# Attention, soft mixture of experts and gated layer in one kernel: the first four heads loaded and scaled in two halves

## The chip, the cores and the metric

The kernel runs on one core of a Trainium2 chip. The metric is the device time of one execution in microseconds (us); the runs shown are executions of the same program, and their median is what is compared.

## The reference, cut to what matters

Three layers follow each other. The first is causal attention over 4 batches, 12 heads, 448 positions and 64 channels a head; its output is the token matrix x of 1,792 rows and 768 columns. The second is a soft mixture of 8 experts with 4 slots each; the third is a gated layer.

```python
scores = scale * np.matmul(q, k.transpose(0, 1, 3, 2))
scores = np.where(mask, -1000000000.0, scores)
scores = scores - np.max(scores, axis=-1, keepdims=True)
attn = np.exp(scores)
attn = attn / (np.sum(attn, axis=-1, keepdims=True) + 1e-09)
return np.matmul(attn, v).astype(np.float32)
...
logits = x @ phi
...
slot_input = d.T @ x
...
    h = np.maximum(slot_input[e] @ w1[e], 0.0)
    slot_out[e] = h @ w2[e]
...
return (c @ slot_out).astype(np.float32)
...
gate = 1.0 / (1.0 + np.exp(-(x @ w_gate)))
val = x @ w_val
return (gate * val @ w_out).astype(np.float32)
```

Here d and c are the softmax of the logits over the tokens and over the slots.

## The kernel before, in words

**The attention stage.** The 48 heads are taken in 24 pairs of two heads (indices i), and the pairs in 12 groups of four heads (indices g, two pairs each). The q, k and v of a group are loaded together: `load` (L270) issues one DMA for each of the four chunks of positions `CH` (128, 128, 128 and 64 rows), each bringing all four heads of the group, 256 bytes a row and head. All loads are issued by SP, in the order of the program. q and k have two buffers for the groups in turn (`qkbuf`, L263), and so has v (`vbuf`, L260).

Scores are computed in half precision from q and k split into a high and a low part. Before the split q and k are multiplied by a power of two, so that they fit. That power comes from the mean square of the group's q and k: `scales` (L287) sums the squares, averages them over the partitions with a small matmul by a constant matrix `avgb` (tile `psq`), and makes from it `qks`, the two factors for q and k, and `sc`, the factor for the scores, with four small DVE operations on `qkp`. For group 0 the squares are summed by one operation on DVE for q and one on ACT for k, each over all 1,024 columns of the group (tile `sq`, sums in `am`). For every later group POOL squares and adds in halves (tiles `sq`, `sqr`).

A pair then passes these steps: `st_T` (L336) transposes q and k on PE into PSUM (`psT`, four matmuls each); `st_hi` (L343) on ACT writes the high part `hi` with the scale; `st_lo` (L347) on DVE writes the rest, `lo`; `score` (L356) multiplies the parts on PE into `psS`, for the blocks of queries t = 0 to 3 (1 and the short last block 3, called Z, in one step, 2 and 0 in the next); `st_m` (L380) on DVE adds the mask, scales and takes the maximum `nm`; `st_e` (L392) on ACT takes the exponential `P` and its sum; `st_r` and `st_ri` (L399, L405) make the reciprocal `r` of the sums on POOL and DVE; `st_P` and `st_C` transpose P on PE (`psP`) and copy it to SBUF; `st_V` multiplies with v, and further steps normalise, transpose and multiply with `phi`.

**What sets the order.** The order in the attention stage is written out by hand: each step of each pair has a time in the table `AT` (L82), each load one in `LOADS` (L86), each part of `scales` one in `SCALES` (L87); `at` and `gen` (L584, L587) put them on a list, which is sorted by time and then written out (L627). `Pinned` (L235) keeps each instruction in this order on its engine; since it calls all of them, most rows of the attention stage carry its line, L244, and are told apart by their tiles. Only the order comes from the table; an instruction runs when its engine has done those before it and its inputs are there. For group 0 all loads and the whole scale stand before time 0, ahead of the transposes of pair 0. The exponential's table is loaded by the operation on `warm` (L626) ahead of the whole list.

**After the attention** a stage streams the experts' weights `w1`, `w2` in 1.5 MB pieces through a ring of buffers, of which ten pieces came during the attention (`load_w`, L173); then the gated layer runs in six parts: per part the weights are converted (`from_f64`, L186, on ACT and DVE; `prep`, L711), gates are computed (`gate`, L834) and the output products are added up in `oacc` (`outp`, L854). The order of these two stages is laid out by the scheduler, which starts from the whole program.

## Time and profile before

| what | value |
|---|---|
| runs | 594.41, 592.43, 593.85 us; median 593.85 |
| profiled execution | span 595.0 us, the time that it has |
| busy share of the span | PE 86%, DVE 66%, ACT 54%, POOL 40% |
| DMA | 101.59 MB, mean 171 GB/s |
| chain that ended last | PE 63%, ACT 15%, DMA 7%, DVE 5%, issue 3%, POOL 2% |

The profiled execution is one run of the program with the hardware profiler; its own time is the span, from the first instruction to the last, and it lies 1.2 us above the median of the runs. PE is TensorE's matmuls, PEld its weight loads, DVE VectorE, ACT ScalarE, POOL GpSimd, SP SyncE. An engine's busy share is taken over the whole span and mixes stages. The chain is followed back from the last instruction, at each step to what released it.

### The profile page before, as it was taken

The numbers are of one execution on the slowest core, as the hardware profiler recorded it, in microseconds if no ns is written. First come the engines' busy times: TensorE is split into PE (matmuls) and PEld (weight loads), VectorE is DVE, ScalarE is ACT, GpSimd is POOL, SyncE is SP. The second block draws the span as 40 slices with busy tenths as digits, with TensorE's granted clock in tenths as the row PEclk, the third lists the DMA queues.
The fourth block names the chain that finished last, engine by engine and source line by source line (L and its number), as shares of the span: only waits on it lengthen the run. The fifth ranks groups of instructions, "written<-read, shape, count | busy, mean of one in ns | idle before, by whom it ended". The sixth has DMA issues, their size and how long they took to land.

```text
span 595.0 us, 12947 instructions
## 1 busy us (share of the span) xinstructions
PE 514.5 (86%) x4971; PEld 317.2 (53%) x4971; DVE 390.0 (66%) x943; ACT 322.6 (54%) x738; POOL 238.7 (40%) x333
## 2 busy tenths in 40 slices
PE   2899989998999899799935689679999989899997
PEld 1576756665667566465512235344554445455654
DVE  3688877886878687331027038986895958675664
ACT  2577767776777577301043049996865843334300
POOL 6654663656365410000000014206696760355720
PEclk9899999999999899979995789998999979799999
DMA  7746557464774313779999993713505303000044
GB/s 161 200 106 170 167 160 199 129 144 133 199 196 115 91 33 107 287 251 391 405 397 405 405 400 137 281 38 119 200 1 209 110 2 107 0 1 1 2 185 186
DMA packets 95566, 101.59 MB, mean 171 GB/s; under 512 B 68625, under 2 KB 68625, under 8 KB 95505
## 3 DMA queue, kind: packets, MB, share of 16 engines
q1 hardware_dynamic: 95504, 100.77, 51.3%
q8 instruction: 39, 0.64, 0.5%
q14 instruction: 23, 0.18, 0.1%
HBM read 95.26 MB, written 5.51 MB: 169 GB/s over the span
## 4 chain that ended last, share of the span: by engine, by line
PE 63%; ACT 15%; DMA 7%; DVE 5%; issue 3%; POOL 2%; SPq 1%; ACTq 0%; DVEq 0%; POOLq 0%
PE pso L870 22%; PE psP L244 9%; PE psS L244 8%; DMA w<-in_moe_w_dram 6%; ACT P L244 4%; PE psX L244 4%; PE psT L244 4%; PE psh L762 3%; PE so L775 3%; ACT hi L244 3%; ACT oacc L144 2%; ACT w L194 2%; PE psg L688 2%; PE psg L843 1%; ACT w L144 1%
## 5 line engine op out<-in xcount | busy, mean ns | idle before, releaser
L852 POOL TENSOR_TENSOR hlo<-hs,hhi 128x448 f16<-128x448 f32 x48 | 59.2, 1241 | 174.9 <-DVE hhi L851 132.5
L870 PE MATMUL pso<-wh,hhi 128*128 128x384 f16 (+1 forms) x384 | 111.5, 338 | 8.1 <-ACT oacc L144 7.6
L870 PE MATMUL pso<-wl,hhi 128*128 128x384 f16 (+1 forms) x384 | 110.3, 334 | 0.0
L870 PE MATMUL pso<-wh,hlo 128*128 128x384 f16 (+1 forms) x384 | 107.8, 331 | 2.6 <-POOL hlo L852 2.6
L244 ACT ACTIVATE P<-psS,nm 128x256 f32<-128x256 f32 (+3 forms) x168 | 82.0, 504 | 31.4 <-PE psP L244 16.6
L870 PEld LDWEIGHTS <-hhi 128*128 128x128 f16 (+1 forms) x768 | 63.5, 103 | 63.8 <-issue 32.3
L244 DVE CUSTOM_DVE_ANT_0 psS<-psS,cmaskq,sc 128x256 f32<-128x256 f32 (+1 forms) x144 | 66.5, 489 | 32.7 <-PE psS L244 30.2
L882 DVE SCALAR_TENSOR_TENSOR oacc<-pso,osc,oacc 128x384 f32<-128x384 f32 x98 | 58.7, 613 | 35.1 <-PE pso L870 34.6
L244 PE MATMUL psP<-ident,P 128*128 128x128 f32 x384 | 59.6, 288 | 17.7 <-ACT P L244 11.6
L880 POOL TENSOR_TENSOR oacc<-oacc,ev 128x384 f32<-128x384 f32 x42 | 55.0, 1321 | 23.1 <-ACT ev L144 23.0
L244 PEld LDWEIGHTS psP<-ident,P 128*128 128x128 f32 x384 | 41.3, 142 | 35.9 <-ACT P L244 21.5
L244 POOL TENSOR_TENSOR sq<-sq 128x512 bf16<-128x512 bf16 (+1 forms) x88 | 56.3, 640 | 6.5
L244 PE MATMUL psV<-PT,v 128*64 128x64 f32 (+3 forms) x672 | 48.0, 293 | 0.3 <-ACT PT L244 0.3
L870 PEld LDWEIGHTS <-hlo 128*128 128x128 f16 (+1 forms) x384 | 34.1, 102 | 26.1 <-issue 3.5
L198 DVE SCALAR_TENSOR_TENSOR w<-w 128x1536 int32<-128x1536 int32 x18 | 33.7, 1874 | 14.5 <-ACT w L144 14.1
L244 PEld LDWEIGHTS psV<-PT,v 128*64 128x64 f32 x672 | 32.0, 137 | 20.9 <-issue 14.0
L144 ACT ACTIVATE ev<-pso,osc 128x384 f32<-128x384 f32 x42 | 23.6, 581 | 27.4 <-PE pso L870 23.7
L194 ACT ACTIVATE w<-w 128x1536 int32<-128x1536 uint16 x18 | 30.2, 1680 | 14.9 <-DMA w<-in_moe_w_out_dram 7.9
L244 POOL TENSOR_SCALAR r<-sum 128x7 f32<-128x7 f32 x24 | 5.9, 244 | 79.1 <-ACT P L244 71.9
L762 PE MATMUL psh<-w,slotT 128*32 128x256 f32 x384 | 29.9, 441 | 7.8 <-DMA w<-in_moe_w_dram 7.3
L244 ACT ACTIVATE hi<-psT,qks 128x448 f16<-128x448 f32 x48 | 27.8, 630 | 15.2 <-PE psT L244 15.2
L770 ACT COPY hT<-psht 128x256 f32<-128x256 f32 x8 | 3.0, 372 | 61.0 <-PE psht L768 61.0
(233 smaller groups left out, 1000.7 us busy)
## 6 DMA issues: line engine op xcount, KB each, us to landing
w<-in_moe_w_dram SPq DMA_DIRECT2D x32, 1536.0 KB, 9.3
w<-in_moe_w_out_dram SPq DMA_DIRECT2D x6, 1536.0 KB, 12.2
w<-in_moe_w_val_dram SPq DMA_DIRECT2D x6, 1536.0 KB, 13.4
w<-in_moe_w_gate_dram SPq DMA_DIRECT2D x6, 1536.0 KB, 6.7
out_dram<-oacc SPq DMA_DIRECT2D x14, 384.0 KB, 2.3
q<-in_q_dram SPq DMA_DIRECT2D x36, 128.0 KB, 3.0
k<-in_k_dram SPq DMA_DIRECT2D x36, 128.0 KB, 2.9
v<-in_v_dram SPq DMA_DIRECT2D x36, 128.0 KB, 8.0
```

Source lines behind the costliest of these rows:

```text
L144: nc.scalar.activation(out=out, in_=in_, func=AF.Copy, scale=x)
L194: nc.scalar.activation(out=lo, in_=top, func=AF.Copy, scale=2.0 ** -13, bias=2.0 ** -15 - 0.5)
L198: nc.vector.scalar_tensor_tensor(lo, hi, -2 ** 31, lo, ALU.bitwise_and, ALU.bitwise_or)
L244: x = f(*a, **kw)
L688: nc.tensor.matmul(ps[32 * g:32 * g + 32, :], lhsT=soT[:, kc], rhs=w[:, kc], start=kc < 4, stop=kc + 4 >= KC)
L762: nc.tensor.matmul(ps[32 * g:32 * g + 32, :], lhsT=slotT[:, kc, :], rhs=w[:, kc % 3, 256 * g:256 * g + 256], start=kc == 0, stop=kc == KC - 1)
L775: nc.tensor.matmul(so[32 * c:32 * c + 32, :], lhsT=hT[:, i, 32 * g:32 * g + 32], rhs=w[:, f % 4, 256 * c:256 * c + 256], start=e == 0 and ...
L843: nc.tensor.matmul(pg, lhsT=d["g"][:, cols], rhs=cT[:, b * S:(b + 1) * S], start=True, stop=True)
L852: nc.gpsimd.tensor_tensor(lo[:, c], hs, hi[:, c], ALU.subtract)
L870: nc.tensor.matmul(ps[n][o:o + m], lhsT=hid[b, u][x][:, c, s0:s0 + m], rhs=y[:, c, 384 * n:384 * n + 384], start=f, stop=l)
L880: nc.gpsimd.tensor_tensor(a, a, x, ALU.add)
L882: nc.vector.scalar_tensor_tensor(a, ps[n], osc, a, ALU.mult, ALU.add)
```

## The change

It touches the attention stage's start only.

- Group 0's q and k are no longer loaded with four heads a DMA. Heads 0 and 1 (o = 0) come first, with four DMAs for q on SP and four for k on ACT's queue, then heads 2 and 3 (o = 2) with eight DMAs on SP.
- `scales` for group 0 runs twice, once for each pair of heads, on half the columns: for o = 0 at times -16 and -15, for o = 2 at 7.0 and 9.4, which is inside pair 0. The squares are written to `vbuf[1]`, which no load has filled yet, in place of the tile `sq`. The steps read the scale of their own pair (`scale_of`).
- The transposes of pair 0 stand at -17, ahead of the first scale.
- The last two parts of group 1's scale stand 3 and 3.4 units later (-1.0 and 0.5 in place of -4.0 and -2.9, relative to that group).
- The table load for the exponential stands at -20 on ACT, behind the four DMA issues there.

```diff
--- before.py
+++ after.py
@@ -275,30 +275,38 @@
 
         def load_q(g):
             grp[g] = {"qk": qkbuf[g % 2]}
-            load(qkbuf[g % 2][0], q, g)
+            if g == 0:
+                for o in (0, 2):
+                    for w, src in enumerate((q, k)):
+                        for j, (s0, n) in enumerate(CH):
+                            (ac if w and not o else sp).dma_start(
+                                out=qkbuf[0][w][:n, j, o * D:(o + 2) * D].rearrange("p (h d) -> p h d", d=D),
+                                in_=src[0, o:o + 2, s0:s0 + n, :].rearrange("h p d -> p h d"))
+            else:
+                load(qkbuf[g % 2][0], q, g)
 
         def load_k(g):
-            load(qkbuf[g % 2][1], k, g)
+            if g:
+                load(qkbuf[g % 2][1], k, g)
 
         def load_v(g):
             grp[g]["v"] = vbuf[g % 2]
             load(vbuf[g % 2], v, g)
 
-        def scales(g):
+        def scales(g, o=None):
 
             n = 4 * HG * D
             if g == 0:
                 am = sm_p.tile([128, 2], F32, tag="am", name="am")
-                for i in range(2):
-                    x = grp[g]["qk"][i].rearrange("p j f -> p (j f)")
-                    sq = qk_p.tile([128, n], BF16, tag="sq", name="sq")
-                    if i:
-                        ac.activation(out=sq, in_=x, func=AF.Square, accum_out=am[:, i:i + 1])
-                    else:
-                        ve.tensor_tensor_reduce(out=sq, in0=x, in1=x, scale=1.0, scalar=0.0, op0=ALU.mult, op1=ALU.add,
-                                                accum_out=am[:, i:i + 1])
+                sq, sk = (vbuf[1].rearrange("p j f -> p (j f)")[:, n // 4 * i:n // 4 * i + n // 4].bitcast(BF16) for i in range(2))
+                j4 = lambda x: x.rearrange("p (j f) -> p j f", j=4)
+                x, y = (grp[g]["qk"][i][:, :, o * D:(o + 2) * D] for i in range(2))
+                ac.activation(out=j4(sk), in_=y, func=AF.Square, accum_out=am[:, 1:2])
+                ve.tensor_tensor_reduce(out=j4(sq), in0=x, in1=x, scale=1.0, scalar=0.0, op0=ALU.mult, op1=ALU.add,
+                                        accum_out=am[:, 0:1])
                 am16 = sm_p.tile([128, 2], BF16, tag="am16", name="am16")
                 ve.tensor_copy(am16, am)
+                yield
                 ps = psT.tile([128, 2], F32, tag="t", name="psq")
                 te.matmul(ps, lhsT=avgb, rhs=am16, start=True, stop=True)
                 mx = ps
@@ -330,8 +338,13 @@
             ve.tensor_scalar(p, p, 2.0 ** (64 + 3 - 14), 2.0 ** -34, ALU.mult, ALU.max)
             ve.reciprocal(s, p)
             ve.tensor_scalar(sc, p[:, 0:1], p[:, 1:2], -scale, ALU.mult, ALU.mult)
-            grp[g].update(s=s, sc=sc)
-            yield
+            for x in range(4) if o is None else (o, o + 1):
+                grp[g]["s", x], grp[g]["sc", x] = s, sc
+            yield
+
+        def scale_of(i, x="s"):
+            g, o = GOF[i]
+            return grp[g][x, o]
 
         def st_T(i, w):
 
@@ -342,12 +355,12 @@
 
         def st_hi(i, w):
             hi = pr[i]["hi", w] = qT_p.tile([128, S], F16, tag=f"hi{w}", name=f"hi{w}")
-            ac.activation(out=hi, in_=pr[i]["ps", w][:, :S], func=AF.Copy, scale=grp[GOF[i][0]]["s"][:, w:w + 1])
+            ac.activation(out=hi, in_=pr[i]["ps", w][:, :S], func=AF.Copy, scale=scale_of(i)[:, w:w + 1])
 
         def st_lo(i, w):
             d = pr[i]
             lo = d["lo", w] = qT_p.tile([128, S], F16, tag=f"lo{w}", name=f"lo{w}")
-            ve.scalar_tensor_tensor(lo, d.pop(("ps", w))[:, :S], grp[GOF[i][0]]["s"][:, w:w + 1], d["hi", w], ALU.mult, ALU.subtract)
+            ve.scalar_tensor_tensor(lo, d.pop(("ps", w))[:, :S], scale_of(i)[:, w:w + 1], d["hi", w], ALU.mult, ALU.subtract)
 
         def scores(i, ts):
             for t in ts:
@@ -386,7 +399,7 @@
             n = ps.shape[1]
             mask = cmask if t == NQ else cmaskq
             c = 2 * t + h
-            ve.tensor_tensor_reduce(out=ps, in0=ps, in1=mask[:, mask.shape[1] - n:], scale=grp[GOF[i][0]]["sc"],
+            ve.tensor_tensor_reduce(out=ps, in0=ps, in1=mask[:, mask.shape[1] - n:], scale=scale_of(i, "sc"),
                                     scalar=3.0e38, op0=ALU.add, op1=ALU.min, accum_out=d["nm"][:, c:c + 1])
 
         def st_e(i, t, h):
@@ -593,7 +606,7 @@
             t0 = II * i
             for w in range(2):
                 x = "qk"[w]
-                at(t0 + AT["T" + x], st_T, i, w)
+                at(t0 + AT["T" + x] if i else -17.0, st_T, i, w)
                 at(t0 + AT["h" + x], st_hi, i, w)
                 at(t0 + AT["l" + x], st_lo, i, w)
             at(t0 + AT["S20"], scores, i, (2, 0))
@@ -619,11 +632,15 @@
             at(t0 + LOADS["q"], load_q, g)
             at(t0 + LOADS["k"], load_k, g)
             at(t0 + LOADS["v"], load_v, g)
-            gen([t0 + x for x in SCALES], scales, g)
+            if g:
+                gen([t0 + x for x in (SCALES if g > 1 else SCALES[:-2] + (-1.0, 0.5))], scales, g)
+            else:
+                gen([-16.0, -15.0], scales, 0, 0)
+                gen([7.0, 9.4], scales, 0, 2)
             if 1 <= g <= NC + NA:
                 at(t0 + LOADS["w"], load_w)
+        at(-20.0, lambda: ac.activation(out=warm, in_=one1, func=AF.Exp))
         at(1.0, lambda: sp.dma_start(out=phis, in_=phi.rearrange("(k p) s -> p k s", p=128)))
-        nc.scalar.activation(out=warm, in_=one1, func=AF.Exp)
         for _, _, f, a in sorted(steps, key=lambda x: x[:2]):
             f(*a)
 
```

What this makes of the order of instructions is shown at three places.

*PE at the program's start.* `psq` is the averaging matmul (avgb its weights, am the sums of squares), `psT` the transposes of pair 0, `psS` its first scores. Before:

```order
L244 LDWEIGHTS avgb
L244 MATMUL psq<-am_178,avgb 128x2
L244 MATMUL psT<-ident,q_150 128x128 x4
L244 MATMUL psT<-ident,k_151 128x128 x4
L244 LDWEIGHTS hi_218
```

And with the change:

```order
L244 MATMUL psT<-ident,q_150 128x128 x4
L244 MATMUL psT<-ident,k_151 128x128 x4
L244 LDWEIGHTS avgb
L244 MATMUL psq<-am_194,avgb 128x2
L244 LDWEIGHTS hi_224
```

The averaging matmul moved behind the eight transposes. On PE a second one, for heads 2 and 3, stands further down between the k transposes of pair 1 and the transposes of pair 0's P.

*DVE inside pair 0,* from the maxima of the second head of score block 1 on. `ISA psS,nm` is the masked maximum of a block and `ISA nm` the reading of it; `cmask` belongs to block Z, the one of 384 columns to block 2. Before:

```order
L244 ISA psS,nm<-psS,cmaskq,sc 128x256
L244 ISA nm 128x1
L244 ISA psS,nm<-psS,cmask,sc 128x448
L244 ISA nm 128x1
L244 ISA psS,nm<-psS,cmaskq,sc 128x384
L244 ISA nm 128x1
```

And with the change:

```order
L244 ISA psS,nm<-psS,cmaskq,sc 128x256
L244 ISA nm 128x1
L244 ISA v_145,am<-q_150 128x512
L244 ISA am 128x1
L244 CAST am_263<-am 128x2
L244 ISA psS,nm<-psS,cmask,sc 128x448
L244 ISA nm 128x1
L244 TENSOR_SCALAR qkp<-psq 128x2
L244 TENSOR_SCALAR qkp<-qkp 128x2
L244 RECIPROCAL qks<-qkp 128x2
L244 TENSOR_SCALAR sc<-qkp 128x1
L244 ISA psS,nm<-psS,cmaskq,sc 128x384
```

Seven operations came in: the squares and their cast ahead of block Z, and the four small operations on the averaging matmul's result ahead of block 2.

*ACT at the start of the gated layer.* `sg` is a sigmoid, `hhi` a high part, `w` a weight tile under conversion, `oacc` an eviction of an output product. Before:

```order
L849 ACTIVATE sg<-psg_5204 128x448
L144 ACTIVATE oacc<-pso,osc_5069 128x384 x4
L194 ACTIVATE w<-w 128x1536
L144 ACTIVATE w<-w 128x1536
L849 ACTIVATE sg<-psg_5283 128x448
```

And with the change (17 lines were added above, so L849 is now L866):

```order
L866 ACTIVATE sg<-psg_5224 128x448
L194 ACTIVATE w<-w 128x1536
L144 ACTIVATE w<-w 128x1536
L144 ACTIVATE oacc<-pso,osc_5089 128x384 x4
L866 ACTIVATE sg<-psg_5303 128x448
```

The scheduler put a weight tile's two conversions ahead of four evictions; the first four of the layer's six parts have more such exchanges, on all engines.

## Rows read from the trace of the kernel before

**Rows 1.** The page: span; the chain that ended last, share of the span by engine.

```profile
span 595.0 us, 12947 instructions
...
PE 63%; ACT 15%; DMA 7%; DVE 5%; issue 3%; POOL 2%; SPq 1%; ACTq 0%; DVEq 0%; POOLq 0%
```

**Rows 2.** Chain of waits, 20 to 56 us: start us, us, what.

```profile
22.75 1.88 PE psS L244 x18
...
32.30 1.02 PE psS L244 x18
...
40.73 1.02 PE psS L244 x18
```

**Rows 3.** Windows: us, busy us of PE, PEld, DVE, ACT, POOL; clock, DMA share, GB/s.

```profile
23.00:24.00 1.00, 1.00 (x16) 0.62 (x10) 0.91 (x5) 0.38 (x1) 0.85 (x3) 0.50 0.89 229
270.00:280.00 10.00, 10.00 (x137) 5.75 (x135) 1.74 (x5) 1.81 (x4) 0.00 (x0) 1.00 1.01 386
380.00:390.00 10.00, 6.23 (x40) 3.86 (x42) 10.00 (x12) 10.00 (x14) 1.65 (x1) 1.00 0.78 305
```

**Rows 4.** Timeline of SP's DMA issues: start us, us, engine, line, operation, count.

```profile
0.74 0.43 SPq L244 DMA_DIRECT2D q<-in_q_dram  x1
...
3.08 2.35 SPq L244 DMA_DIRECT2D k<-in_k_dram  x4
```

**Rows 5.** DMA issues, first 12 us: operation, count, KB each, median us to landing.

```profile
k<-in_k_dram SPq DMA_DIRECT2D x6, 128.0 KB, 3.1
...
q<-in_q_dram SPq DMA_DIRECT2D x2, 64.0 KB, 2.9
```

**Rows 6.** Timeline, first scale: start us, us, engine, line, operation [idle before <-releaser].

```profile
0.73 1.28 ACT L626 ACT_TABLE_LOAD   x1 [0.73 <-PEq L943]
...
7.96 1.06 ACT L244 ACTIVATE sq<-k 128x1024 bf16<-128x1024 f32 x1 [5.73 <-DMA k<-in_k_dram]
...
9.14 0.17 DVE L244 CAST am<-am 128x2 bf16<-128x2 f32 x1 [2.36 <-ACT sq L244]
...
9.37 0.16 PE L244 MATMUL psq<-am,avgb 128*128 128x2 bf16 x1 [9.37 <-DVE am L244]
...
10.35 1.06 PE L244 MATMUL psT<-ident,k 128*128 128x128 f32 x4
10.35 0.17 DVE L244 RECIPROCAL qks<-qkp 128x2 f32<-128x2 f32 x1
...
11.44 1.16 ACT L244 ACTIVATE hi<-psT,qks 128x448 f16<-128x448 f32 x2 [2.33 <-PE psT L244]
```

**Rows 7.** Timeline, pair 0's second half: PE, DVE, ACT.

```profile
15.33 0.47 ACT L244 ACTIVATE P<-psS,nm 128x256 f32<-128x256 f32 x1 [2.73 <-DVE nm L244]
...
18.13 1.12 PE L244 MATMUL psT<-ident,k 128*128 128x128 f32 x4
18.36 0.63 DVE L244 CUSTOM_DVE_ANT_0 psS<-psS,cmaskq,sc 128x384 f32<-128x384 f32 x1 [1.84 <-PE psS L244]
...
19.28 1.16 ACT L244 ACTIVATE hi<-psT,qks 128x448 f16<-128x448 f32 x2 [2.93 <-PE psT L244]
```

**Rows 8.** Timeline: POOL's squares and row sum, DVE behind them.

```profile
9.25 2.04 POOL L244 TENSOR_TENSOR sq<-q 128x512 bf16<-128x512 f32 x2 [3.80 <-ACT sq L244]
...
22.97 0.26 POOL L244 TENSOR_SCALAR r<-sum 128x7 f32<-128x7 f32 x1 [3.18 <-ACT P L244]
...
24.48 0.20 DVE L244 RECIPROCAL r<-r 128x8 f32<-128x8 f32 x1
...
24.78 0.69 DVE L244 CUSTOM_DVE_ANT_0 psS<-psS,cmask,sc 128x448 f32<-128x448 f32 x1
...
27.80 0.63 DVE L244 CUSTOM_DVE_ANT_0 psS<-psS,cmaskq,sc 128x384 f32<-128x384 f32 x1 [2.26 <-PE psS L244]
```

**Rows 9.** Timeline of ACT in the gated layer: two weight conversions.

```profile
362.46 1.68 ACT L194 ACTIVATE w<-w 128x1536 int32<-128x1536 uint16 x1
363.99 1.64 ACT L144 ACTIVATE w<-w 128x1536 f32<-128x1536 f32 x1
```

## The prediction

> **What bounds the kernel now.** I read the page first, then the chain of waits, then the first 30 us in order of time, because all that the change writes lies there. The page's chain [rows 1] says that TensorE (PE) is the engine that sets the end: 63% of the chain, ACT 15%, DMA 7%. The stages differ. The attention stage (to about 250 us) is a loop over pairs of heads in which one pair follows the other at 8.43 us (32.30 to 40.73 in [rows 2]); after it comes a stretch in which the weights stream in with the DMA engines full (share 1.01, [rows 3]), whose buffers are freed by the matmuls of the attention's end; after that the gated layer, ACT-bound in its first 40 us (10.00 us busy of 10, [rows 3]) and then PE-bound. No stage has a clock of its own: each starts when the one before lets it. So a time taken off the start should come off the end, if the loop is not held by something else in its first rounds.
>
> In the start PE does no work that counts before 9.37 us. SP issues four DMAs for q and four for k, 0.59 us each (2.35 / 4, [rows 4]), the last k chunk lands 2.9 to 3.1 us after its issue [rows 5], and ACT's Square of k can begin only at 7.96 [rows 6]. Then a chain runs: Square and its sum until the DVE cast at 9.14, the averaging matmul at 9.37, four small DVE operations until the scale stands at 10.52 (10.35 + 0.17), beside it eight transposes on PE, and ACT's first hi at 11.44, waiting for the last transpose, not for the scale [rows 6]. From that hi on one pair hangs on the last.
>
> **The change part by part.**
>
> 1. *The first two heads ahead.* q and k of heads 0 and 1 are now four DMAs on SP and four on ACT, both starting near 0.74. At SP's spacing the fourth begins at 0.74 + 3 x 0.59 = 2.5, and with 3.0 us to landing both are there at 5.5 instead of 7.96. ACT's table load now follows its issues; it takes 1.28 us [rows 6] and ends near 4.5, under the cover of that landing (without the cover it would add at most its length). No row has an issue on ACT. The low bound is 0.43 us an issue, SP's first [rows 4]: landed at 5.0. The high one is that the eight issues go one after another as now: 8.0. I take 5.5, the value nearest to the rows of a queue by itself.
>
> 2. *Half the Square.* 1,024 columns and their sum take 1.18 us (7.96 to 9.14, [rows 6]); 512 columns save half of the 1.06: 0.65 us, so am stands near 6.2 and the cast is done by 6.4. The same holds for q on DVE, which ends sooner.
>
> 3. *Transposes first.* The first three q transposes run as their chunks land; from 5.5 on the last q one and four of k remain. Four take 1.06 us from the first's start to the last's end [rows 6], five by that some 1.5 with the pass from q to k (an estimate): the k set ends near 7.0. The averaging matmul, now behind them on PE, starts at about 6.8 instead of 6.4 and costs 0.4 there. From it to the scale it is 1.15 us (9.37 to 10.52): the scale stands at 7.95, and hi begins at 8.1 instead of 11.44. **Lead: 3.3 us.** The bounds of step 1 make it 3.8 and 1.3.
>
> 4. *A second scale for heads 2 and 3, inside pair 0.* It adds one Square on ACT (0.65), one on DVE with a cast (about 0.9), one matmul and four small DVE operations. SP's eight extra issues follow its first four and end near 8.2, so k's last chunk lands near 10.8; ACT's Square runs until 11.5 in the gap between hi and the first exponential, which is now 2.73 us long [rows 7]; that exponential is wanted at 15.33 - 3.3 = 12.0, so it fits. The DVE part stands before the mask of score block 4 alone, which nobody awaits early. What costs is the wait: in DVE's queue the four scale operations now stand before the maxima of score block 2, and they wait for a matmul that PE reaches only after the next pair's k transposes. Now those maxima start at 18.36 and the k transposes at 18.13, the hi after them at 19.28 [rows 7]. With the scale's 1.15 us counted from the last transpose's start (about 18.85), the scale stands at 20.0 in today's times and hi of pair 1 begins there, **0.7 late**; the maxima begin near 20.0 too, 1.65 late, but ACT works at that hi for 1.16 us meanwhile, so the exponentials and PE behind them are late by ACT's 0.7 and no more. Behind the maxima in DVE's queue stands lo of pair 1, which PE needs only after those exponentials' transposes. Bounds: nothing (if the matmul slips in during the transposes) and 1.65.
>
> 5. *The group behind.* POOL's squares of group 1 wait for a q that SP now issues after twelve DMAs, not eight, and a reused semaphore holds SP some 0.5 us: start 11.9 instead of 9.25. Their 10.54 us of work (from 9.25 to 3.18 before 22.97, [rows 8]) end at 22.4. Behind them in POOL's queue stands the row sum r of pair 0, wanted at 22.97 - 2.6 = 20.4 [rows 8]; it is done by 22.95, so DVE's reciprocal is 1.1 late (wanted 24.48 - 2.6 = 21.9). DVE then has that reciprocal (0.20), a mask (0.69) and the moved scale of group 1, under 1.15, and reaches the next maxima at 25.0; these are wanted at 27.80 - 2.6 = 25.2 [rows 8]. The cover holds with 0.2 us to spare, so I cost it at nothing; each tenth that the loads slip beyond this goes on the path. The scale of group 1 itself moved to a later slot and is needed only by pair 2. The first v and phi come 2.4 us later and are used after 25 us.
>
> Sum: 3.3 - 0.7 = **2.6 us**. It is worked in the profiled execution, whose span is 595.0 us [rows 1], so that one would be 592.4; the runs of the kernel before have a median of 593.85, and the forecast on it is 593.85 - 2.6 = **591.2 us**. The bounds of 1 and 4 alone give 590.0 to 594.2 (lead 3.8 and no cost; lead 1.3 and 1.65). A measurement here tells 0.3%, or 1.8 us, from no change.
>
> **Rivals.**
>
> *A. The two queues do not run side by side.* Then k is there at 7.96, as in [rows 6]. Still half a Square (0.53) and the transposes out of the way (hi at 10.1 instead of 11.44) are won, 1.3 us, and 0.7 is paid: 593.85 - 0.6 = 593.2, no change. For it: [rows 4] show issues at an even 0.59 us, as a stage that both queues share would set them. Against it: SP is one engine that issues in order, which explains the same row. [...]
>
> *B. The clock rises later: slower.* [...] The change puts a wait of DVE between the two bursts of PE work in pair 0. If the rise comes a whole pair later in the work, a pair of 8.43 us with PE on 63% of the chain [rows 1] costs 0.84 x 0.63 x 8.43 = 4.5 us (0.84 is 1.88 / 1.02 - 1): 593.85 - 2.6 + 4.5 = 595.7. It is slower than before from a rise 4.9 us late on. Against it: the matmuls before and behind that wait are the same ones in the same order.
>
> *C. The gated layer's order.* The order there is laid out anew by the scheduler. On ACT the second pair of weight conversions (362.46 and 363.99, [rows 9], 3.0 us to the next operation) now stands ahead of four evictions, and PE's banks wait that long. ACT is full there either way, so I expect nothing; if PE does not make it good it gives the 3.0 back: 594.2, and more if two units do it. Other shifts of that layer may win as much.
>
> *D. The clock rises one burst earlier,* since PE now works from about 3.6 us on (0.74 + 2.9): 0.86 for the score step [rows 2] and about as much for the transposes behind it: 589.5.
>
> **How the numbers follow.** The forecast has 0.52, A 0.18, C 0.13, B 0.09, D 0.08. Faster: forecast and D, 0.60. Slower by over 0.3%: B's upper part, 0.06, and C's, 0.05: 0.11. Within: A, the rest of C and B: 0.29. The forecast's own range is 590.0 to 592.0; to hold 8 in 10 it must take in A and most of C, and part of D: 589.2 to 594.8.
>
> **What would show it.** Right: k's Square near 5.5, the first hi near 8.1, the hi of pair 1 some 2.6 us before 19.28, PE's score steps from then on about 2.6 early, the weights' full stretch and the last output shifted alike. A: ACT's four issues longer than 0.59 us each or alternating with SP's, Square near 8. Step 4 wrong: hi of pair 1 waits for the scale by more or less than 0.7. Step 5 wrong: DVE is not done with pair 1's mask and the scale by 25.2. B or D: the window in which the clock leaves 0.50, counted from the first score matmul. C: attention ends early, but the gated layer lasts longer than now.

## The result, and the profile after

The changed kernel takes 587.69 us (median of 4 runs, 587.01 to 588.09) against 594.13 us (4 runs, 592.43 to 597.25): a ratio of 0.9884, 95% interval 0.985 to 0.9918. Timed once more beside the experiments it was 585.9 us and 0.9845 (0.9808 to 0.9883). The forecast was 591.2 us with a range from 589.2 to 594.8: it had the sign right, but the time came out 3.5 us lower, below the range. Two executions far out are in no median and no ratio here, one of the kernel before (1211.71 us) and one in a run of the section on the start (659.85 us at a granted clock of 0.745).

One number must be set right first. A run of the changed kernel that took 587.01 us has a span of 585.0 us; the time is the span plus 2.0. So the profiled execution of before, with a span of 595.0 us, was not 1.2 us above the median but a run of some 597, as slow as the slowest that was timed. Profiled once more, the kernel before has a span of 592.3 us, and the readings below use that second trace too.

The page of the changed kernel, its span and the chain (compare [rows 1]): PE's share has fallen from 63% to 53%, while DMA and DVE have come up.

```profile
span 585.0 us, 12976 instructions
...
PE 53%; ACT 16%; DMA 13%; DVE 8%; issue 5%; POOL 3%; SPq 1%; ACTq 0%; POOLq 0%; DVEq 0%
```

The chain of waits of the changed kernel, pairs 2 and 3 (compare [rows 2]): the score steps stand 2.49 us earlier than in the first trace of before, and the pace from one to the next, 8.43 us, is the same.

```profile
29.81 1.02 PE psS L244 x18
38.24 1.02 PE psS L244 x18
```

The 2.49 holds for this pair of traces only. In the second trace of before and in the second one of the changed kernel the first of these two steps stands here:

```profile
30.80 1.02 PE psS L244 x18
```

```profile
29.51 1.02 PE psS L244 x18
```

That is a lead of 1.29 us. Over the five traces of the old start that are used below, the first matmul of this step lies between 30.73 and 32.23 (median 31.50), over five of the new start, with the changed kernel's order of loads and scales, between 29.44 and 29.74 (median 29.52): by the medians the start wins 2.0 us at pair 2.

Two windows of the changed kernel (compare [rows 3]): the weights' stretch is as full as before, and ACT as busy in the gated layer.

```profile
270.00:280.00 10.00, 10.00 (x152) 5.83 (x148) 1.11 (x3) 0.91 (x2) 0.00 (x0) 1.00 1.03 396
380.00:390.00 10.00, 6.59 (x36) 3.34 (x35) 9.74 (x15) 10.00 (x16) 0.00 (x0) 1.00 0.34 130
```

The start of the changed kernel in order of time (compare [rows 4, 6, 7, 8]; start us, us, engine, line, operation, idle before and what ended it):

```profile
0.74 4.52 SPq L244 DMA_DIRECT2D q<-in_q_dram  x8
0.74 2.26 ACTq L244 DMA_DIRECT2D k<-in_k_dram  x4
...
5.35 0.63 ACT L244 ACTIVATE v<-k 128x512 bf16<-128x512 f32 x1 [0.82 <-DMA q<-in_q_dram]
6.11 0.17 DVE L244 CAST am<-am 128x2 bf16<-128x2 f32 x1 [0.35 <-ACT v L244]
6.33 0.16 PE L244 MATMUL psq<-am,avgb 128*128 128x2 bf16 x1
6.93 0.17 DVE L244 RECIPROCAL qks<-qkp 128x2 f32<-128x2 f32 x1
7.19 1.16 ACT L244 ACTIVATE hi<-psT,qks 128x448 f16<-128x448 f32 x2 [1.11 <-DVE qks L244]
...
11.45 2.44 POOL L244 TENSOR_TENSOR sq<-q 128x512 bf16<-128x512 f32 x2 [5.55 <-DMA q<-in_q_dram]
...
16.18 1.16 ACT L244 ACTIVATE hi<-psT,qks 128x448 f16<-128x448 f32 x2 [4.08 <-DVE qks L244]
...
22.46 0.24 POOL L244 TENSOR_SCALAR r<-sum 128x7 f32<-128x7 f32 x1
...
22.98 0.20 DVE L244 RECIPROCAL r<-r 128x8 f32<-128x8 f32 x1 [0.90 <-POOL r L244]
...
25.39 1.16 ACT L244 ACTIVATE hi<-psT,qks 128x448 f16<-128x448 f32 x2 [1.02 <-DVE qks L244]
```

Two queues issue side by side, 12 DMAs in 4.52 us. The first hi begins at 7.19 instead of 11.44, a lead of 4.25. The hi of pair 1 begins at 16.18 and now waits for the scale, the row that `qks` names; DVE's reciprocal of pair 0 waits for POOL's row sum; the hi of pair 2 begins at 25.39. What is left of 4.25 at the score step of pair 2 is 2.5 us in these two traces, close to the forecast of 2.6, and 2.0 by the medians above. The other 4 us of the gain are not in the start.

### The profile page after: what moved, and what is told of

Its sections match the earlier page's. It is cut to its first block, busy times and chain, and to the rows that moved or that the text cites. A ratio compares the mean times of both kernels' runs of the same rounds, so it can differ in the third digit from the quotient of the medians.

```text
span 585.0 us, 12976 instructions
## 1 busy us (share of the span) xinstructions
PE 505.0 (86%) x4972; PEld 312.7 (53%) x4972; DVE 391.8 (67%) x950; ACT 323.0 (55%) x740; POOL 243.1 (42%) x333
## 4 chain that ended last, share of the span: by engine, by line
PE 53%; ACT 16%; DMA 13%; DVE 8%; issue 5%; POOL 3%; SPq 1%; ACTq 0%; POOLq 0%; DVEq 0%
PE pso L887 18%; PE psP L244 8%; PE psS L244 7%; DMA w<-in_moe_w_gate_dram 6%; ACT P L244 4%; PE psX L244 4%; PE psT L244 4%; DMA w<-in_moe_w_val_dram 3%; DMA w<-in_moe_w_dram 3%; ACT w L144 3%; PE psh L779 3%; ACT hi L244 2%; PE so L792 2%; ACT w L194 2%; POOL sq L244 2%
## 5 line engine op out<-in xcount | busy, mean ns | idle before, releaser
L887 PE MATMUL pso<-wh,hhi 128*128 128x384 f16 (+1 forms) x384 | 109.3, 333 | 6.1 <-DVE hhi L868 3.0
L887 PE MATMUL pso<-wl,hhi 128*128 128x384 f16 (+1 forms) x384 | 108.1, 330 | 0.0
L887 PE MATMUL pso<-wh,hlo 128*128 128x384 f16 (+1 forms) x384 | 106.1, 329 | 2.2 <-POOL hlo L869 2.1
L887 PEld LDWEIGHTS <-hhi 128*128 128x128 f16 (+1 forms) x768 | 62.3, 102 | 60.2 <-issue 24.9
L897 POOL TENSOR_TENSOR oacc<-oacc,ev 128x384 f32<-128x384 f32 x42 | 57.5, 1385 | 27.6 <-ACT ev L144 27.3
L792 PE MATMUL so<-w,hT 128*32 128x256 f32 x384 | 31.1, 395 | 5.4 <-DMA w<-in_moe_w_dram 3.8
```

What stands on the lines that cost most here:

```text
L792: nc.tensor.matmul(so[32 * c:32 * c + 32, :], lhsT=hT[:, i, 32 * g:32 * g + 32], rhs=w[:, f % 4, 256 * c:256 * c + 256], start=e == 0 and ...
L887: nc.tensor.matmul(ps[n][o:o + m], lhsT=hid[b, u][x][:, c, s0:s0 + m], rhs=y[:, c, 384 * n:384 * n + 384], start=f, stop=l)
L897: nc.gpsimd.tensor_tensor(a, a, x, ALU.add)
```

## Where the rest comes from: order against start

The scheduler lays out the order behind the attention anew when the attention changes. To tell order and start apart, both kernels were built with the order of the other: the sequence in which each engine issues its instructions behind the attention was recorded from one kernel and laid on the other, as dependencies of order only. The attention itself keeps the order in which it is written.

```diff
+    later = nc.cur_bb.bb.instructions[traced:]
+    for engine, code in RECORDED.items():
...
+        for a, b in zip(seq, seq[1:]):
+            tc.add_manual_dep(b, a.name, mybir.DependencyInfo(mybir.DependencyClass.NoSync, mybir.DependencyReason.DATA),
+                              reason="recorded order")
```

All runs that follow carry such a record, but for the two kernels repeated unchanged.

**Before, again.**

> The kernel before, unchanged, profiled and timed once more, to see which parts of its first profile come back. Theory 1 (the gain behind the attention is the new order of the gated layer): the same stage lengths as in its first profile from 260 us on, about 594 us. Theory 2 (the gain comes from falls of TensorE's clock that the first profile of the kernel before had, at 203 to 206 us and in the gated layer, and the new one had not): the falls come back at the same places, since the kernel is the same. Theory 3 (they are chance of one execution): the fall at 203 us is missing, and the span is nearer to 591 to 592.

**After, again.**

> The changed kernel unchanged, timed beside the others: about 587.7 us under every theory, span about 585.7; ratio to the kernel before 0.989.

**New start, old order.**

> The changed kernel's attention, and behind it every engine's order of the kernel before. Theory 1 (the re-laid order of the gated layer gave what the start did not, some 3.9 us): 591.5 us, the forecast of the start alone. Theory 2 (the start gave it all, by 2.5 us of lead and by a clock that does not fall later): 587.7 us, as the changed kernel.

**Old start, new order.**

> The kernel before's attention, and behind it every engine's order of the changed kernel. Theory 1: 594.1 - 3.9 = 590.2 us. Theory 2: 594.1 us, no change. If order and start each need the other (a clock that falls or not by where in time a wait comes), this and the run before it do not add up to the whole.

Measured, with the gated layer's part read from each trace (from the first psv, its first value product, to the end of the span; the median is over all runs of a kernel, the span that of the one run with a trace):

| start | order | median us | ratio to before, 95% interval | span us | first psv at | from there to the end |
|---|---|---|---|---|---|---|
| old | old | 594.01 | 0.9982 (0.9955 to 1.0008) | 592.3 | 348.10 | 244.2 |
| new | old | 592.11 | 0.9950 (0.9923 to 0.9978) | 591.1 | 346.94 | 244.2 |
| old | new | 589.60 | 0.9917 (0.9888 to 0.9945) | 586.6 | 350.54 | 236.1 |
| new | new | 585.90 | 0.9845 (0.9808 to 0.9883) | 584.1 | 348.18 | 235.9 |

The start alone is worth about 2 us (594.01 to 592.11), or 3.7 with the new order behind it, and the order alone some 4.4; together they give 8.1 here. The 1.7 us by which the whole exceeds the two parts are no more than the intervals allow. Of the two crossed runs theory 1 holds, and theory 2 falls: the gated layer is 8 us shorter with the new order, whichever start stands ahead of it. Some of that is paid earlier: from the attention's last step (its first psm, at 247.66, 246.36, 248.35 and 246.26 in the table's sequence) to the first psv the new order takes 1.3 to 1.8 us more. The recorded order itself changes nothing that the traces show: 244.2 and 236.1 with a record are the 244.2 and 235.9 of the kernels without one. The fall of the clock at 203 us (0.50 from 204 to 207 us in the first trace of before) is absent from the second trace of before, whose score steps there are 11.32 us apart (198.42 and 209.74) against 12.95 in the first: theory 3 of the first run is right about that one. In the first traces the score steps before and after it are 2.47 us apart (199.96 and 197.49) and 4.20 us behind it (212.91 and 208.71), so it cost that execution 1.7 us. The falls in the gated layer come back at the same places (near 474 and 505 us), with the same order: the mean clock is 0.83 from 464 to 484 us in both traces of before, and 0.81 and 0.72 from 500 to 512.

## What in the order

The names in the rows: hs is gate times value, made on DVE from the value product psv, in two halves; hhi and hlo are its high part and the rest; pso is an output product, which is either added into oacc by DVE, or copied to ev by ACT and added by POOL.

TensorE's waits and POOL's queue in the second trace of before, 463 to 507 us:

```profile
463.04 3.42 POOL L880 TENSOR_TENSOR oacc<-oacc,ev 128x384 f32<-128x384 f32 x2 [2.99 <-ACT ev L144]
466.42 1.04 POOL L852 TENSOR_TENSOR hlo<-hs,hhi 128x448 f16<-128x448 f32 x1
468.26 4.15 POOL L880 TENSOR_TENSOR oacc<-oacc,ev 128x384 f32<-128x384 f32 x2 [0.80 <-ACT ev L144]
472.37 2.54 POOL L852 TENSOR_TENSOR hlo<-hs,hhi 128x448 f16<-128x448 f32 x1
...
474.97 1.60 PE L870 MATMUL pso<-wh,hlo 128*64 128x384 f16 x4 [2.16 <-POOL hlo L852]
...
506.36 0.74 PE L844 MATMUL psv<-cT,st 128*128 128x448 f32 x1 [2.38 <-DVE hs L850]
```

The second half of one hlo stands behind two additions into oacc in POOL's queue, 4.15 us, and TensorE waits 2.16 us for it. The windows of the same trace (us, busy us of PE with count, granted clock, DMA share, GB/s) show what follows each of the two waits: the granted clock is lower for a time, so that the mean of the stretch is 0.83 and 0.72. Behind the first wait one shape of matmul (128x384, f16) starts every 0.32 us from 477.46 to 480.34, and every 0.16 from 481.13 on.

```profile
464.00:484.00 20.00, 16.77 (x86) 0.83 0.00 1
500.00:512.00 12.00, 8.90 (x32) 0.72 0.00 0
```

The changed kernel, second trace, in the same windows: no loss in the first. In the second the granted clock is lower for a time too, 0.86 in the mean (the same shape starts every 0.32 us from 501.45 to 502.09, and every 0.16 from 506.28 on).

```profile
464.00:484.00 20.00, 19.29 (x132) 1.00 0.03 4
500.00:512.00 12.00, 12.00 (x73) 0.86 0.00 0
```

What stands ahead of that fall, just before the window, is a wait of its own, its longest there, for a cast hhi on DVE:

```profile
499.17 0.50 PE L887 MATMUL pso<-wh,hhi 128*128 128x384 f16 x2 [2.50 <-DVE hhi L868]
```

Windows at fixed times compare different work, since the changed kernel is ahead. The starts of TensorE's matmuls, counted from the first psv on (1,398 in every trace), do not have this fault. The table gives the us from the first psv to the matmul that comes so many later; its last four rows are the runs that follow:

| trace | 650 | 700 | 850 | 900 | end |
|---|---|---|---|---|---|
| before, second | 117.2 | 130.3 | 152.8 | 168.4 | 244.2 |
| changed, second | 116.3 | 123.9 | 146.0 | 160.2 | 235.9 |
| one move in the old order | 118.9 | 129.3 | 150.5 | 164.9 | 240.7 |
| both waits of the old order | 116.6 | 127.0 | 148.2 | 161.0 | 236.8 |
| the wait put back | 116.3 | 131.9 | 153.0 | 168.1 | 244.0 |
| the new order's own wait | 116.7 | 124.4 | 146.3 | 158.6 | 234.4 |

Of the changed kernel's 8.3 us, 0.9 are won in the first 650 matmuls, 5.6 in the next 50, where POOL's hlo is waited for, 1.5 from 850 to 900, where each kernel has its other wait, and nothing behind that.

Four runs test whether these waits carry the gain, by one or a few moves in a recorded order.

**One move in the old order.**

```diff
 POOL hlo<-hs,hhi     (first half)
+POOL hlo<-hs,hhi     (second half)
 POOL oacc<-oacc,ev
 POOL oacc<-oacc,ev
-POOL hlo<-hs,hhi     (second half)
```

> The kernel before with its own recorded order, and one POOL instruction moved: the second half of hlo of one unit stands ahead of the two oacc additions that it stood behind (in the kernel before TensorE waits 2.16 us for it near 475 us, and its clock is at half until about 482). Theory 1a (the wait and the fall of the clock that follows it are what the new order saves): the wait goes, the fall near 475 to 482 us goes with it, and 2.2 + 3.4 = 5.6 us at most are won, some 589.5 us. Theory 1b (the new order wins by many small shifts): 593 to 594 us, and the wait comes back at a neighbour. Between them: the 2.2 us alone, 592.

Measured: 590.87 us, ratio 0.9948 (0.9926 to 0.997). Between the two theories' times: 3.1 us against 594.01. In the trace, which is of the slowest of these runs (594.14 us), the wait for hlo is gone and a smaller one for an eviction stands in its place, and the clock of that stretch holds; the 50 matmuls take 10.4 us instead of 13.1:

```profile
480.19 0.32 PE L882 MATMUL pso<-wh,hhi 128*128 128x384 f16 x1 [1.44 <-ACT ev L155]
```

```profile
464.00:484.00 20.00, 17.99 (x111) 1.00 0.23 79
500.00:512.00 12.00, 8.99 (x39) 0.86 0.00 0
```

**Both waits of the old order.**

```diff
 DVE hs     (first)
 DVE oacc<-pso,osc,oacc
 DVE oacc<-pso,osc,oacc
+DVE hs     (second)
+DVE hhi<-hs
 DVE w<-w   (last half of a weight conversion)
...
-DVE hs     (second)
-DVE hhi<-hs
```

> The kernel before with its own recorded order and both of its long waits of TensorE in the gated layer taken down by one move each: POOL's second half of hlo ahead of two additions (as in the run with that alone), and DVE's second hs and the cast hhi ahead of the last half of a weight conversion (TensorE waits 2.4 us for that hs near 506 us, the clock at half behind it). Theory 1a (these two waits and the falls of the clock behind them are what the new order is worth): the gain of the new order, 4.7 us, or more: 589.5 or less. Theory 1b (the new order is worth more than its two waits): 591, as with the first move alone.

Measured: 586.91 us, ratio 0.9876 (0.9838 to 0.9914), with the old start. That is as much as the new order gives (589.60 with the old start), from three moved instructions: theory 1a. It is not won at the same places: the two moves save 2.7 us at the first wait and 2.8 at the second, the new order 5.6 and 1.5.

**The wait put back into the new order.**

```diff
-POOL hlo, oacc, oacc, hlo (second half), oacc, oacc
+POOL oacc, oacc, hlo, oacc, oacc, hlo (second half)
```

> The changed kernel with its own recorded order, but POOL's six instructions around that hlo in the sequence of the kernel before, so that the half of hlo stands behind the two additions again. Theory 1a: TensorE waits for it some 2 us near 467 us, with or without a fall of the clock behind it: 2.0 to 5.5 us more than the changed kernel, 588 to 591. Theory 1b: in the new order other instructions stand differently, and TensorE is not waiting there: 586.

Measured: 593.06 us, ratio 0.9974 (0.9948 to 1.0001). Six instructions on POOL take back the whole gain of the change, and more than the 5.5 us allowed for. TensorE reaches that matmul earlier in the new order and waits more than twice as long; the 50 matmuls take 15.5 us instead of 7.6, and what the changed kernel had won by then is gone:

```profile
467.16 3.49 POOL L909 TENSOR_TENSOR oacc<-oacc,ev 128x384 f32<-128x384 f32 x2 [1.45 <-ACT ev L155]
470.61 1.03 POOL L881 TENSOR_TENSOR hlo<-hs,hhi 128x448 f16<-128x448 f32 x1
471.69 0.53 PE L899 MATMUL pso<-wh,hlo 128*64 128x384 f16 x1 [5.24 <-POOL hlo L881]
```

```profile
464.00:484.00 20.00, 14.29 (x79) 0.83 0.00 1
```

**The new order's own wait.**

```diff
 DVE hs     (first)
+DVE hhi<-hs
 DVE oacc<-pso,osc,oacc
 DVE oacc<-pso,osc,oacc
+DVE hs     (second)
-DVE w<-w   (last half of a weight conversion)
...
 DVE oacc<-pso,osc,oacc
-DVE hhi<-hs
-DVE hs     (second)
 DVE oacc<-pso,osc,oacc
+DVE w<-w   (last half of a weight conversion)
```

> The changed kernel with its own recorded order, and three DVE instructions moved: the cast hhi right behind its hs, the second hs ahead of the last half of a weight conversion, and that half (1.75 us) behind two evictions (in the changed kernel TensorE waits 2.5 us for hhi near 499 us and its clock is at half for some 2.9 us behind it). Theory 1a: most of the wait (1.9 of 2.5) and the fall (half of 2.9) go: 3.3 us less than the changed kernel, about 583. Rival: the conversion moved is waited for later, or evictions come late by it: no gain, 586.

Measured: 584.37 us, ratio 0.9844 (0.982 to 0.9868), against 0.9845 for the changed kernel: the interval does not tell it apart. In the trace the wait is 0.53 us instead of 2.50, and the mean clock from 500 to 512 us is 1.00 instead of 0.86:

```profile
498.37 0.32 PE L899 MATMUL pso<-wh,hhi 128*128 128x384 f16 x1 [0.53 <-DVE oacc L911]
```

The place behaves as expected, and this trace is 1.5 us shorter from the first psv on; that the kernel as timed is faster by it is not shown.

## What in the start

Each of these carries the changed kernel's recorded order behind the attention, so the gated layer is the same.

**One queue.**

```diff
-(ac if w and not o else sp).dma_start(
+sp.dma_start(
```

> The changed kernel with its own recorded order behind the attention, and k of the first two heads issued on SP too, behind q's four. Theory (two queues run side by side, and POOL's squares of group 1 set the pace of pair 2): four issues of 0.57 us more on SP, the first hi near 9.4 instead of 7.1, POOL's squares at 13.4 instead of 11.1 and the hi of pair 2 near 27.4 instead of 25.1: 2.3 us more than the changed kernel, 588. Rival A (the queues share one stage): no difference, 586.

Measured: 588.57 us, ratio 0.9914 (0.9881 to 0.9946). The first hi, POOL's squares and the hi of pair 2 are all late, the last by 1.7 us against the changed kernel's 25.39:

```profile
8.69 1.16 ACT L255 ACTIVATE hi<-psT,qks 128x448 f16<-128x448 f32 x2 [1.11 <-DVE qks L255]
...
13.55 2.04 POOL L255 TENSOR_TENSOR sq<-q 128x512 bf16<-128x512 f32 x2 [7.71 <-DMA q<-in_q_dram]
...
27.08 1.16 ACT L255 ACTIVATE hi<-psT,qks 128x448 f16<-128x448 f32 x2 [1.89 <-DVE qks L255]
```

Rival A of the prediction is out: without the second queue 2.7 of the start's 3.7 us are gone.

**The group whole, on two queues.**

```diff
-                for o in (0, 2):
...
-                            (ac if w and not o else sp).dma_start(
+                        (ac if w else sp).dma_start(out=qkbuf[0][w][:n, j].rearrange("p (h d) -> p h d", d=D),
+                                                    in_=src[0, :4, s0:s0 + n, :].rearrange("h p d -> p h d"))
...
-gen([t0 + x for x in (SCALES if g > 1 else SCALES[:-2] + (-1.0, 0.5))], scales, g)
+gen([t0 + x for x in SCALES], scales, g)
...
-gen([-16.0, -15.0], scales, 0, 0)
-gen([7.0, 9.4], scales, 0, 2)
+gen([-16.0, -15.0], scales, 0)
```

> The changed kernel with its own recorded order behind the attention, but group 0 whole: q's four DMAs on SP, k's four on ACT, 128 KB each, one scale for four heads, and group 1's scale at the slots of the kernel before. Transposes first, as in the change. Theory (two queues and the transposes bring the lead, splitting the group brings 0.5 us at the first hi and costs 1.2 at the second and more at POOL): the first hi near 7.7 instead of 7.2, no wait at hi of pair 1, POOL's squares of group 1 at 9.2 or before instead of 11.45, so pair 2 is 0.5 to 1.5 us earlier than in the changed kernel: 585. Rival (halves are needed: eight DMAs of 128 KB at once land later than 5.5): the first hi at 9 or later, 587 to 588.

Measured: 587.9 us, ratio 0.9914 (0.9886 to 0.9942): the rival. ACT issues its four DMAs of 128 KB in 2.37 us, against 2.26 for four of 64 KB, but the squares that wait for the data begin at 7.56 and 7.78 instead of 5.05 and 5.35, and the first hi at 10.34:

```profile
0.74 2.37 ACTq L255 DMA_DIRECT2D k<-in_k_dram  x4
7.56 1.22 DVE L255 CUSTOM_DVE_ANT_0 v<-q 128x1024 bf16<-128x1024 f32 x1 [5.04 <-DMA q<-in_q_dram]
7.78 1.06 ACT L255 ACTIVATE v<-k 128x1024 bf16<-128x1024 f32 x1 [3.15 <-DMA q<-in_q_dram]
...
10.34 1.16 ACT L255 ACTIVATE hi<-psT,qks 128x448 f16<-128x448 f32 x2 [1.42 <-DVE qks L255]
```

So the halves are what makes the data land early, beside the queues: with two queues alone the square of k begins at 7.78, hardly ahead of the 7.96 and 7.64 in the two traces of before.

**The second scale earlier.**

```diff
-gen([7.0, 9.4], scales, 0, 2)
+gen([7.0, 9.015], scales, 0, 2)
```

> The changed kernel with its own recorded order behind the attention, and the second scale's matmul and its four DVE operations at 9.015 instead of 9.4, which is ahead of k's transposes of pair 1. Theory (step 4: the scale is late because its matmul stands behind those transposes): hi of pair 1, which began at 16.18 in the changed kernel's profile, begins near 15.1, 1.0 us earlier, and the score steps from pair 2 on move by the same. Rival (POOL's row sum r and group 1's scale set the pace behind it): hi of pair 1 moves by 1.0, and pair 2 not at all. Time: 585.0 or 586.0.

Measured: 585.75 us, ratio 0.9864 (0.9838 to 0.9889). The hi of pair 1 begins 2.2 us earlier than in the changed kernel's first trace, more than the 1.0 of the theory: in this execution TensorE's matmuls were at full speed inside pair 0 already (four k transposes in 0.64 us at 13.17, against 1.12 at 13.87). That of pair 2 begins only 0.3 earlier, and no earlier than in the second trace (25.09), because POOL's row sum has hardly moved (22.20 against 22.46 and 22.16):

```profile
14.00 1.16 ACT L255 ACTIVATE hi<-psT,qks 128x448 f16<-128x448 f32 x2 [2.16 <-DVE qks L255]
...
22.20 0.24 POOL L255 TENSOR_SCALAR r<-sum 128x7 f32<-128x7 f32 x1
...
25.13 1.16 ACT L255 ACTIVATE hi<-psT,qks 128x448 f16<-128x448 f32 x2 [3.07 <-DVE qks L255]
```

The rival holds. The wait for the second scale is real and costs nothing at pair 2: POOL does.

**Transposes behind the scale again.**

```diff
-at(t0 + AT["T" + x] if i else -17.0, st_T, i, w)
+at(t0 + AT["T" + x], st_T, i, w)
```

> The changed kernel with its own recorded order behind the attention, and pair 0's transposes behind the first scale's matmul again. Theory (pair 2 waits for POOL, so what pair 0 wins beyond that is lost again): the first hi near 8.3 instead of 7.1, the hi of pair 2 at 25.1 as in the changed kernel, 586. Rival (step 3's lead goes through to the end): 587.2.

Measured: 585.63 us, ratio 0.986 (0.9823 to 0.9897). The time is that of the theory, but the trace is not: the first hi is at 8.39 as expected, and the hi of pair 2 at 26.49, 1.1 later than in the changed kernel. In that execution one of group 1's q chunks also landed late (POOL's second square waited 0.48 us for it), and the granted clock was 0.50 from 18 to 24 us. The trace decides nothing, and the interval, some 2 us to either side, holds the rival's time too.

**Group 1's q ahead.** The loads in the sequence in which they are issued, with half(queue, w, o) for the four DMAs of q (w = 0) or k (w = 1) of heads o and o + 1:

```diff
 half(sp, 0, 0)
 half(ac, 1, 0)
 half(sp, 0, 2)
+load(qkbuf[1][0], q, 1)
 half(sp, 1, 2)
-load(qkbuf[1][0], q, 1)
 load(qkbuf[1][1], k, 1)
...
-gen([7.0, 9.4], scales, 0, 2)
+gen([7.7, 9.4], scales, 0, 2)
```

> The changed kernel with its own recorded order behind the attention, and group 1's q issued on SP ahead of k of heads 2 and 3, the squares of the second scale at 7.7 instead of 7.0 (behind the first two exponentials). Theory (POOL's squares of group 1, which begin when their q lands, set pair 2): they begin near 8.8 instead of 11.1, wait 0.8 for k, end 1.5 earlier, and the hi of pair 2 begins near 23.6 instead of 25.1: 1.5 us less than the changed kernel, 584.4. Rival (the second scale, now later, holds pair 1 and with it pair 2): the hi of pair 1 at 16.5 or later, pair 2 at 25.1, 586.

**The same, with hhi early.**

> Both at once: group 1's q ahead, and DVE's hhi and second hs of the last but one part ahead of the half conversion. If both theories hold the gains add: 1.5 of the run with group 1's q ahead and the 1.5 that the run with hhi early measured: 583.

**The same start, with the repaired old order.**

> The start with group 1's q ahead, and behind the attention the kernel before's order with both waits taken down. If the start and the order add: 586.9 for that order with the old start, less 2.2 for the changed start, less 1.8 for group 1's q: 582.9, the fastest of all. Rival (the order laid out for the changed start suits it better): 584 or more, as the other two with this start.

Measured: 584.06 us, ratio 0.9829 (0.9796 to 0.9862), the lowest median of all, 584.41 us, 0.9843 (0.9806 to 0.9881), and 585.97 us, 0.9863 (0.9823 to 0.9903). POOL's squares begin at 9.06 and its row sum at 20.09, 2.4 us earlier than in the changed kernel, but the hi of pair 2 came at 24.93 in the first run, 0.5 earlier, and at 23.61 in the second, whose start is the same program. The two part ahead of POOL: the four k transposes of pair 1 took 1.12 us at 13.88 in the first and 0.66 at 13.62 in the second, and its hi began at 16.15 and 15.01. The first run's rows:

```profile
9.06 2.13 POOL L255 TENSOR_TENSOR sq<-q 128x512 bf16<-128x512 f32 x2 [3.63 <-DMA q<-in_q_dram]
...
20.09 0.25 POOL L255 TENSOR_SCALAR r<-sum 128x7 f32<-128x7 f32 x1
...
24.93 1.16 ACT L255 ACTIVATE hi<-psT,qks 128x448 f16<-128x448 f32 x2 [0.64 <-PE psT L255]
```

Against the changed kernel's 0.9845 none of the three is told apart by its interval, and in the third the gains of start and order do not add up as expected. A version that surely beats the change was not found.

## Why the prediction was wrong, point by point

- **Steps 1 to 3, the lead.** 4.25 us instead of 3.3. The data were there at 5.05 to 5.35, between the low bound (5.0) and the value taken (5.5). The averaging matmul was taken to wait for the transposes until 6.8; it ran at 6.33, right behind the cast. From it to the scale it took 0.77 us (6.33 to 6.93 + 0.17) where 1.15 was carried over from [rows 6]: one of the four small DVE operations took 0.55 us there (at 9.76) and 0.17 here. Each of the three errors pointed the same way. Against the second trace of before (11.12) the lead is 3.9.
- **Step 4, the second scale.** 0.7 late was forecast; the first trace has hi of pair 1 at 16.18 where 19.28 - 4.25 = 15.03 was open to it, 1.15 late, inside the bounds. The mechanism is as described, but it is no term of the sum: moved out of the way, it gave pair 2 0.3 us against one trace of the changed kernel and nothing against the other.
- **Step 5, POOL.** Forecast: squares start at 11.9, r by 22.95, no cost with 0.2 us to spare. Measured: 11.45 and 22.46. SP was held 0.2 us, by a wait for a DMA of k, not 0.5. With the larger lead the cover was gone, and DVE's reciprocal waited for r. Lead 4.25 less what this chain took is 2.5 at pair 2. That the sum of 2.6 nearly came out was luck: two terms were mis-sized in opposite directions, and by the medians of five traces it was 2.0. As a forecast of the start alone it held: with the old order behind it the new start takes 592.11 us, inside the range.
- **Rival C, the step that failed.** The order of the gated layer was costed at "nothing" because ACT is full there either way, and its 3.0 us stood on the losing side with 0.13; of a gain the text only said that other shifts may win as much. Measured, that order is worth 4.4 us with the old start and 6.2 with the new. The argument looked at ACT in the first 40 us of that layer [rows 9]. Most of the gain lies over 100 us later, in POOL's and DVE's queues, where before's trace had two more waits of TensorE over 2 us: one move on POOL took 3.1 us off the old order, both moves together 7.1, and the opposite move in the new order cost 7.
- **Rivals B and D, the clock.** Both start from a clock that rises once, behind pair 0: B's 1.88 and 1.02 us are the score steps at 22.75 and 32.30 [rows 2], and the granted clock was 0.50 from 23 to 24 us [rows 3]. The rows show more than one change. In the second trace of before TensorE's transposes ran at little over half speed in pair 0 (1.11 us for four, against 0.60 at 24.76), at full speed once (0.66), and the clock fell again behind a stretch with no matmul (17.97 to 20.13):

```profile
15.34 1.11 PE L244 MATMUL psT<-ident,q 128*128 128x128 f32 x4
17.31 0.66 PE L244 MATMUL psT<-ident,k 128*128 128x128 f32 x4
```

```profile
8.00:18.00 10.00, 6.79 (x59) 1.00 0.67 146
20.00:22.00 2.00, 1.87 (x9) 0.54 0.92 183
```

The 1.00 of the first window is not what these matmuls ran at. The traces' records of the granted clock begin only at 19.3 and 16.7 us (before) and at 15.1 and 22.3 us (changed), and ahead of the first record the view gives 1.00. In the changed kernel's second trace the windows from 8 to 24 us all say 1.00, and yet TensorE is at half speed until 22 us (the four matmuls of the score row below take 0.43 us, as they do at 20.11 in the first trace with the clock at 0.50, and 0.30 at 29.44):

```profile
11.28 1.11 PE L244 MATMUL psT<-ident,q 128*128 128x128 f32 x4
19.95 0.43 PE L244 MATMUL psS<-hi,hi 64*64 64x256 f16 x4
23.03 0.63 PE L244 MATMUL psT<-ident,q 128*128 128x128 f32 x4
```

The prediction asked for the time from the first score matmul to the clock's lasting rise: it is 11.2 to 13.5 us in those five traces with the old start and 12.9 to 14.4 in the five with the new. So the clock rose neither a burst earlier (D) nor a whole pair of 8.43 us later (B); counted so it rose later by about 1 us at the median.

- **Rival A.** Out, by the rows with both queues at work, which show no loss: 0.57 us an issue on either queue (4.52 / 8 on SP, 2.26 / 4 on ACT), 0.59 for SP alone [rows 4].

## What to carry to other kernels

When a scheduler lays out a part anew, its old order's waits on the bounding engine are the price list: go through each wait over 1 us in the whole trace and ask whether the new order still has it, before costing the part at nothing. A side engine's queue (here POOL, 42% busy) can hold back the bounding engine by one instruction that stands behind two others. And an early lead is worth only what the slowest other chain lets through: trace every engine to the point where they meet again.

## What had not been expected of the hardware

- TensorE's speed in the start differs between executions of one program. The four k transposes of pair 1 took 1.12 us at 18.13 in the first trace of before and 0.66 at 17.31 in the second, and the hi of pair 2 began at 28.26 and 26.76. No run here shows what decides it.
- A granted clock of 1.00 in a profile's first 20 us can mean that no record was there. The duration of matmuls of one shape, early and late (1.11 and 0.63 us), tells the speed.
- The timed runs of before scatter from 590.87 to 597.85 us, about 1%, those of the changed kernel from 584.05 to 588.09 over both sets. A single profile of this kernel can be off by 3 us, as the first one of before was.
- A subtraction on POOL of one and the same shape (hlo, 128 x 448) took 1.04 us at 466.42 and 2.54 at 472.37, in the second trace of before, and TensorE went on only behind the longer one, at 474.97. No run here shows what makes the difference.
